# u read to all partitions by one DMA and kept as bf16, in a linear-attention and long-convolution kernel with a new instruction order

## The chip, the cores and the metric

The kernel runs on one core of a Trainium2 chip. The metric is the device time of one launch in microseconds, as the median over several runs. A core has five engines that work at the same time, each through its own list of instructions in order: PE (TensorE, matmuls), DVE (VectorE), ACT (ScalarE), POOL (GpSimd) and SP (SyncE, which here issues every DMA). Matmul results land in PSUM, which POOL can't read; all else lies in SBUF.

## What is computed

The inputs r, k, v and w have the shape 4 x 8 x 768 x 48 (batch, heads, steps, width of a head), and u is 8 x 48. For each batch and head a 48 x 48 state runs through the steps, and its output goes through a projection, a circular convolution over the 768 steps with a gate on each side, and an output projection:

```
cur   = outer(u * k[t], v[t])
y[t]  = r[t] @ (state + cur)
state = w[t][:, None] * state + outer(k[t], v[t])
...
x1, x2, x3 = split(x @ w_proj)          # x is y with the heads side by side, 768 x 384 per batch
out = (x1 * irfft(rfft(x2) * rfft(filter)) * x3) @ w_out
```

The term with u, called the bonus here, is v[t] times one number per step and head: the sum over the head's width of r[t] * k[t] * u.

## The kernel before

The 768 steps of a batch are cut into six chunks of 128 steps, so there are 24 chunks, numbered 0 to 23 through the four batches. A chunk's r, k, v and w come by one DMA each (ldr, ldk, ldv, ldw), 128 partitions (the steps) by 384 values, of which each run of 48 lies apart in memory. Six buffers of each are used in turn.

Work on a chunk c, by the names of the functions (op_ left out): lw takes the logarithm of w on ACT. cs and ce add it up over the steps by matmuls with a triangular mask (inclusive and exclusive). en and eq, or enp and eqp, which write back into PSUM, take exponentials on ACT. kh or khp makes k times the one and q or qp makes r times the other, on DVE or POOL; those with a p read PSUM and are DVE's. tqk transposes both on PE, tT copies the result, sc multiplies them into scores, and mt masks these on DVE (or ma copies them on ACT and mm masks them on POOL). kv and S carry the state. rk is r * k in bf16, rku is rk * u, cc sums rku over each head on DVE, and vc is v * cc on POOL: the bonus. y multiplies the scores with v and adds the state's share; yb also adds vc by an identity matmul, and its result is copied out by xc, where after a plain y the addition is done by xn on DVE. yt transposes, and xT copies the transposed chunk.

Work on a batch b: sa and sb add and subtract the two halves of the sequence, x2 projects them, ab copies. f does a discrete Fourier transform by matmuls with a table F, in six slots f.b.0 to f.b.5. da and db (or X, ua and ub) multiply the slots with the filter's transform T, pp adds, i1 and i2 transform back, ec, s and d put the halves together. p1 and p3 are the other two projections, taken up by x1 and g (or gc and gm). yy multiplies, po (in the last batch poa and pob) projects the output, o copies it, and st stores it.

Set-up: iota, ang and sin make F. Of these, ang writes into o0 but reads a ramp that lies in the tile `filt`, so the filter's own load (ldfilt) waits until ang and angn are done. fs and fd add and subtract the halves of the filter, hf transforms them (slots 0 and 1 need fs alone, 2 and 3 both, 4 and 5 fd), and ht, hr, he and hb make T from that with small rotations (rot, which rsc scales). mtr, mc and ms make the tables for the way back. ldp loads a third of the projection weights (ldp1 for x2, ldp0 for p1, ldp2 for p3) or the output weights (ldp3), and wc converts them to bf16. z and zs are matmuls on a zero tile whose results aren't used.

u is loaded by ldu (L371) as one row on one partition. us (L324) spreads it to 128 partitions by a matmul with a row of ones, and uc (L328) copies this from PSUM into u_bc, which is FP32 (L193); rku (L552) reads u_bc. um (L331), uv (L339) and hm (L315) make a second form of u that only the functions rt, rT, cu and cv (L559 to L576) read, the bonus by PE. None of these four stands in the order.

The order of everything is the string ORDER (L37 to L129). Each word names an engine, a function and its numbers, and for PE a PSUM bank: `V:rku0`, `A:lw1`, `P:ce1@2`. emit (L855) walks through it, and each engine does its words in this order, waiting only where data or a buffer demands it. One further wait is written in: a POOL word with a `!` waits for the last DVE word ahead of it that is in the set `shut` (L851), which holds operations on SBUF alone. The document calls this wait a turn. Loads and stores are words of SP, so they too go in this order.

Of the kernel before, what the change touches and what calls it, by code (L numbers as in the profile page):

```python
# [42 lines left out]
V:hr0.0 A:ht0.1 A:enp2 G:q1! V:hr0.1 V:tT0 V:rku1 P:zs8@2 P:hf3@0 A:ht1.0 A:he G:v0! P:z2@2 P:mtr0@2
G:rk2! A:ht1.1 A:mc0 P:tqk1@3 P:hf4@1 P:sc0@8 V:hr1.0 V:hr1.1 G:vc0! V:cc1 V:khp2 S:ldr3 S:ldv1
P:kv0@5 A:tT1 A:lw3 V:rku2 G:v1! P:z3@0 P:cs3@4 V:S0 S:ldk3 P:mtr1@0 V:q2 P:ce3@3 A:ht2.1 A:ms0
A:en3 G:kh3! A:eq3 S:ldw4 P:tqk2@2 G:rk3! V:hb0 P:kv1@3 P:hf5@4 V:cc2 A:mc1 A:lw4 A:ht2.0 A:tT2
V:mt0 G:vc1! S:ldw5 S:ldv2 S:ldr4 V:hr2.1 A:lw5 P:sc1@8 S:ldk5 P:zs2@1 P:ce4@5 S:ldk4 P:z3@1 V:S1
A:hb1 V:mt1 G:rku3! P:cs4@3 G:q3! A:eqp4 V:hr2.0 P:zs2@2 P:sc2@8 A:v2 V:mt2 P:cs5@2 S:ldv3 V:qp4
P:yb0@1 A:en5 G:vc2! V:cc3 P:kv2@4 A:en4 A:xc0 P:tqk3@2 A:ph4 G:rk4! P:yt0@1 P:mtr2@3 P:yb1@5 A:tT3
P:sc3@8 P:zs2@2 P:yb2@2 V:kh4 V:S2 V:ms2 P:tqk4@4 G:rku4! S:ldv5 S:ldw6 G:kh5! A:v3 A:mc2 A:xc1  # L50
P:ce5@5 A:xT0 A:hb2 A:eqp5 V:mt3 V:cc4 V:tT4 S:ldv4 P:zs1@1 A:lw6 P:yt1@3 P:kv3@1 A:ms1 G:v5! G:v4!
P:sc4@8 P:ce6@0 S:ldr5 G:rk5! S:ldw8 S:ldr6 V:S3 A:xc2 A:xT1 V:qp5 P:tqk5@2 P:yt2@5 P:kv4@3 A:lw8
A:eq6 S:ldk6 G:vc4! P:ce8@1 P:cs6@4 G:rku5! V:mt4 P:yb4@0 A:tT5 V:S4 S:ldw7 P:sc5@8 A:enp6 A:xc4
G:q6! A:lw7 P:zs1@2 P:cs8@3 V:cc5 A:eq8 A:en8 P:y3@2 V:khp6 G:vc5! S:ldp1 V:xT2 G:vc3! V:mt5 P:yt4@0
# [6 lines left out]
A:tT7 V:S6 P:y6@3 A:v7 V:da0.2 P:cs9@0 G:rk8! A:en9 A:x10.1.0 P:f0.5@2 A:wc2 P:p10.1.1@1 G:vc7!
V:da0.1 V:xn6 V:db0.2 S:ldk9 V:rku8 P:yt6@3 P:p10.0.0@0 P:ce9@5 P:kv7@2 P:sc7@8 A:xT6 V:ub0.1
P:p10.2.0@4 V:pp0.2 V:pp0.1 V:rk9 V:pp0.0 A:eq9 A:x10.0.0 A:x10.2.0 P:p30.1.1@3 A:x10.1.1 P:tqk8@5
A:ma7 V:rku9 G:q9! G:mm7! S:ldk10 V:g0.1.1 P:p30.1.0@0 V:g0.1.0 S:ldv8 V:cc8 P:p30.0.0@4 S:ldw10
V:cc9 V:g0.0.0 A:tT8 A:v8 V:S7 P:i20.2@1 S:ldw11 P:i10.2@3 S:ldr10 P:p10.0.1@0 P:p30.2.0@5 P:sc8@8
P:yb7@4 S:ldr11 A:lw10 A:ec0.2 V:g0.2.0 P:cs10@2 S:ldw12 S:ldv9 G:kh9! S:ldv10 S:ldk11 A:x10.0.1
S:ldw14 G:vc8! S:ldv11 A:lw11 P:kv8@0 P:ce10@5 S:ldk12 S:ldv12 P:i20.1@1 V:d0.2 V:mt8 A:en10 A:xc7
P:ce11@2 P:tqk9@4 A:eq10 S:ldr12 A:ec0.1 A:eqp11 V:s0.2 V:S8 G:rk10! P:y8@5 P:i20.0@1 G:q10! P:yt7@3
S:ldw13 V:xn8 G:kh10! P:i10.1@0 V:qp11 A:tT9 S:ldp3 A:ec0.0 P:sc9@8 A:xT7 V:s0.1 G:rku10! S:ldk13
A:v9 S:ldk14 S:ldv13 S:ldr13 G:vc9! S:ldr14 A:lw12 S:ldw15 P:yt8@2 S:ldw16 S:ldv14 V:d0.1 S:ldk15  # L70
S:ldw17 S:ldr15 P:tqk10@1 A:tT10 P:cs11@3 A:enp11 P:i10.0@4 V:mt9 P:kv9@0 V:xT8 S:ldr16 V:S9
P:p30.0.1@5 P:yb9@1 G:rk11! V:cc10 A:v10 A:xc9 G:yy0.1! P:ce12@2 P:p11.1.0@0 A:eq12 V:khp11
P:p30.2.1@1 P:tqk11@2 P:cs12@3 V:g0.0.1 V:d0.0 P:sc10@8 P:yt9@5 A:x11.1.0 A:lw14 A:v11 A:en12 A:tT11
V:g0.2.1 V:s0.0 P:p11.0.0@0 P:ce14@3 V:sb9 A:eq14 A:v12 P:kv10@4 P:p11.2.0@1 G:vc10! G:rku11!
P:p31.2.0@2 G:kh12! A:x11.2.0 V:mt10 S:ldk16 V:sa9 V:xT9 V:cc11 V:S10 P:yb10@3 G:yy0.2! A:lw13
A:gc1.2.0 A:xc10 V:rk12 S:ldv15 S:ldr17 S:ldk17 S:ldw18 P:x21.1.0@5 A:x11.0.0 V:q12 V:rku12 P:cs14@1
P:ce13@2 S:ldw19 P:yt10@3 P:sc11@8 P:p31.0.0@0 P:cs13@4 A:ab1.1.0 A:eq13 G:vc11! P:x21.0.0@2 V:sb10
G:yy0.0! P:p31.1.0@5 V:mt11 V:sa10 A:xT10 V:g1.1.0 A:en13 A:ab1.0.0 P:tqk12@4 P:y11@2 A:wc3 V:g1.0.0
A:enp14 P:x21.1.1@3 S:ldw20 V:xn11 V:khp14 V:cc12 P:po0.4@5 P:po0.1@0 A:tT12 G:kh13! P:kv12@2
G:rk13! P:po0.5@1 V:S12 V:q14 A:ab1.1.1 A:o0.1 P:yt11@4 A:xT11 V:rku13 V:q13 A:o0.5 A:lw15 P:po0.0@3  # L80
V:sb11 V:sa11 P:tqk14@0 P:p11.0.1@2 P:tqk13@1 S:ldv16 P:sc12@8 G:vc12! P:x21.0.1@4 G:rk14! G:v14!
A:v13 V:tT14 S:ldk18 P:kv13@0 A:o0.4 A:x11.0.1 G:rku14! V:mt12 P:cs15@2 P:x21.0.2@5 V:cc13 A:tT13
A:o0.0 S:ldr18 G:vc13! V:S13 P:ce15@1 A:lw16 A:en15 P:sc13@8 P:po0.3@3 A:eq15 P:kv14@2 P:ce16@0
P:x21.1.2@1 S:ldv17 V:mt13 A:ab1.0.1 P:sc14@8 G:kh15! P:yb13@4 A:lw17 A:o0.3 G:q15! S:ldk20 V:S14
S:ldv18 A:ab1.1.2 P:ce17@1 P:y12@3 A:eq16 P:f1.5@0 G:rk15! V:cc14 S:ldk19 S:ldr20 G:vc14! V:mt14
P:tqk15@2 A:xc13 A:eq17 S:ldr19 V:xn12 A:ab1.0.2 G:rk16! G:q16! S:ldw21 P:cs17@1 P:f1.1@4 P:cs16@3
P:f1.2@5 V:db1.2 S:ldv19 A:tT15 V:db1.0 P:yb14@2 V:da1.1 A:enp16 A:en17 A:xc14 P:p31.2.1@0 P:sc15@8
V:khp16 V:rku15 V:rku16 P:yt14@2 P:yt13@5 P:yt12@1 P:f1.4@4 A:xT14 S:ldk21 A:xT12 A:xT13 P:f1.0@2
A:v15 P:p31.0.1@1 A:gc1.2.1 S:ldr21 P:p32.1.0@5 P:p11.1.1@0 P:p12.2.0@3 V:gm1.2.0 V:da1.2 V:cc15
A:lw19 V:g1.0.1 P:cs19@1 P:f1.3@4 A:lw18 A:gc2.1.0 A:x11.1.1 A:en19 A:x12.2.0 A:lw20 V:da1.0 G:rk17!  # L90
V:mt15 P:p32.0.0@2 G:pp1.2! P:tqk16@0 A:tT16 G:kh17! G:q17! A:v16 P:kv15@1 P:p12.0.0@3 P:p11.2.1@5
A:x12.0.0 V:db1.1 P:tqk17@4 V:rku17 A:tT17 V:pp1.0 V:pp1.1 P:sc16@8 P:po0.2@0 V:S15 P:cs18@3 A:en18
G:vc15! V:g2.0.0 V:cc16 P:ce18@1 P:i21.2@4 P:cs20@3 P:kv16@2 V:mt16 A:eq18 A:ec1.2 V:cc17 G:rk18!
A:en20 S:ldw23 S:ldk22 P:y15@1 G:q18! P:i21.1@4 S:st0.3 S:ldv20 A:x11.2.1 P:sc17@8 P:i21.0@5 G:vc16!
P:ce20@3 V:xn15 V:S16 A:v17 A:ec1.1 V:mt17 P:y16@4 P:yt15@2 A:o0.2 A:ec1.0 V:sa15 G:kh18! V:xT15
V:xn16 A:eq20 P:ce19@0 S:ldw22 P:p32.2.0@5 P:p31.1.1@3 P:y17@1 A:eq19 A:v18 V:g2.2.0 P:tqk18@0
A:tT18 G:kh20! P:yt16@4 V:sb15 G:q20! S:st0.0 S:ldr22 P:i11.1@5 P:x22.0.0@2 V:rku18 G:vc17! A:xT16
S:ldr23 S:ldv22 S:st0.1 S:ldv21 A:ab2.0.0 A:lw21 V:g1.1.1 S:ldv23 S:ldk23 G:rk19! S:st0.4 G:kh19!
V:sb16 P:tqk20@3 P:kv18@0 V:d1.1 P:sc18@8 P:x22.1.1@2 V:sa16 V:s1.1 V:xn17 G:rku19! A:tT20 P:i11.2@4
P:x22.0.1@5 P:yt17@3 V:S18 V:cc18 A:ab2.1.1 V:s1.2 A:v19 A:xT17 P:x22.1.0@0 G:q19! P:i11.0@2  # L100
A:ab2.1.0 A:ab2.0.1 V:sb17 V:d1.2 P:p32.1.1@1 P:ce21@0 P:p12.1.1@5 A:x12.1.1 V:sa17 P:x22.0.2@3
P:cs21@4 A:gc2.1.1 V:mt18 G:rk21! G:rk20! G:vc18! V:d1.0 V:s1.0 A:eq21 V:cc19 P:sc20@8 A:en21 A:lw23
V:yy1.1 V:gm1.2.1 P:x22.1.2@5 P:kv19@1 A:ab2.0.2 V:S19 P:p32.2.1@2 A:gc2.2.1 G:kh21! G:rku20!
P:p32.0.1@4 P:y18@3 A:ab2.1.2 P:tqk19@0 A:v20 V:mt20 A:tT19 A:lw22 P:p12.1.0@5 A:gc2.0.1 P:f2.3@1
P:p12.0.1@2 V:xn18 P:yt18@3 P:sc19@8 A:x12.0.1 A:xT18 A:x12.1.0 P:kv20@0 V:yy1.0 V:yy1.2 P:f2.1@4
P:ce22@2 A:eq22 V:db2.1 V:S20 V:cc20 P:po1.5@3 P:cs23@1 A:en23 V:db2.0 G:q21! P:po1.0@0 P:cs22@2
A:enp22 A:o1.5 P:po1.3@5 V:mt19 P:y20@1 G:rku21! G:vc20! P:tqk21@4 P:f2.4@3 A:o1.0 P:po1.1@0 V:xn20
# [804 lines left out]
```

## Time and profile before

| | |
|---|---|
| median of 3 runs | 158.15 us (158.08 to 158.39) |
| the profiled execution | 159.17 us |
| its span, from the first to the last instruction | 157.5 us |
| mean granted clock of PE | 0.98 of full speed |
| ACT busy | 128.0 us |
| read from memory | 22.41 MB |
| written to memory | 4.72 MB |

How to read the lines of the profile in what follows. In a table of groups each row is a line of the kernel, an engine, an operation and its tiles (output <- inputs, with buffer numbers left out) and the count, then the busy time in us and the mean of one in ns, then the idle time of the engine just before them with what ended most of it. The types in a row are those of the output and of one input only. In a list in order of time a row begins with the start and the duration in us. In the chain of waits (the chain of work that ended last, followed back from the end) a row is a start, a duration and what was done. In a list of waits a row gives who waited for whom, the sum in us, how many times, and the longest. PE's ends are modelled, since matmuls overlap; the chain's durations don't overlap.

### The profile page before, as it was taken

What the parts mean: (1) busy time and instruction counts of PE and PEld (TensorE: products, weight loads), DVE (VectorE), ACT (ScalarE), POOL (GpSimd) and SP (SyncE); (2) the same over time, 40 slices, a digit from 0 to 9 for tenths busy, and PEclk for the clock granted to TensorE, in tenths of its full rate; (3) what the DMA queues carried; (4) which work ended last, traced back from release to release, by engine and by line L of the source; (5) the groups of instructions that cost most, each with busy time, mean ns of one, the idle gap of its engine ahead of it and who ended that gap; (6) DMA issues with size and microseconds to landing.
All of it is one profiled execution on the core that took longest, in us unless ns stands there. A gap on an engine that the chain in (4) does not pass through costs nothing.

```text
span 157.5 us, 4173 instructions
## 1 busy us (share of the span) xinstructions
PE 143.3 (91%) x1553; PEld 92.6 (59%) x1553; DVE 139.1 (88%) x254; ACT 128.0 (81%) x264; POOL 108.7 (69%) x147
## 2 busy tenths in 40 slices
...
GB/s 100 187 320 209 151 201 208 216 172 249 232 176 266 163 211 219 142 251 183 204 229 190 174 205 184 205 242 195 251 14 152 0 102 2 0 0 91 234 241 190
...
## 3 DMA queue, kind: packets, MB, share of 16 engines
...
q8 instruction: 12, 0.20, 0.5%
q14 instruction: 8, 0.07, 0.1%
HBM read 22.41 MB, written 4.72 MB: 172 GB/s over the span
## 4 chain that ended last, share of the span: by engine, by line
PE 46%; DVE 4%; ACT 2%; issue 1%; ACTq 0%
PE p L699 10%; PE po L812 8%; PE i L770 5%; PE f L431 4%; PE x L730 3%; PE tqk L588 3%; PE sc L601 2%; PE f L424 2%; PE y L654 2%; PE yt L677 1%; PE y L649 1%; PE ce L495 1%; PE kv L629 1%; PE cs L489 1%; ACT xT L235 1%; PE kv L627 1%
## 5 line engine op out<-in xcount | busy, mean ns | idle before, releaser
L699 PE MATMUL p<-xT,wproj 128*128 128x384 bf16 x144 | 28.9, 326 | 0.0
L608 DVE TENSOR_TENSOR mt<-sc,mask_excl 128x1024 bf16<-128x1024 f32 x21 | 25.5, 1213 | 0.0
L582 POOL TENSOR_TENSOR vc<-v,cc 128x384 bf16<-128x384 bf16 x24 | 19.9, 831 | 7.3 <-DVE P L764 3.0
L547 POOL TENSOR_TENSOR qk<-ldr,eq 128x384 bf16<-128x384 f32 x16 | 16.1, 1003 | 11.2 <-ACT eq L514 5.5
L550 POOL TENSOR_TENSOR rk<-ldr,ldk 128x384 bf16<-128x384 f32 x21 | 20.9, 1001 | 3.9 <-DMA ldr<-in_r_dram 2.1
L235 ACT ACTIVATE qkT<-tqk 128x1024 bf16<-128x1024 bf16 x21 | 21.7, 1034 | 1.3 <-PE tqk L588 1.2
L699 PEld LDWEIGHTS <-wproj 128*128 128x128 bf16 x144 | 12.7, 97 | 8.2 <-issue 0.8
L588 PE MATMUL tqk<-ident,qk 128*128 128x128 bf16 x192 | 14.8, 219 | 2.6 <-DVE qk L547 1.8
L543 POOL TENSOR_TENSOR qk<-ldk,en 128x384 bf16<-128x384 f32 x14 | 14.0, 1005 | 3.0 <-DVE g L725 1.5
L485 ACT ACTIVATE lg<-ldw 128x384 bf16<-128x384 f32 x24 | 12.8, 539 | 3.9 <-DMA ldw<-in_w_dram 3.7
L730 PE MATMUL x<-wproj,sd 128*128 128x384 bf16 x72 | 14.5, 326 | 1.1 <-POOL wproj L236 0.6
L588 PEld LDWEIGHTS <-qk 128*128 128x128 bf16 x192 | 12.0, 97 | 4.7 <-DVE qk L547 2.0
L770 PE MATMUL i<-m_b,P 128*128 128x384 bf16 x72 | 14.6, 326 | 0.0
L812 PE MATMUL po<-wout,y 128*128 128x384 bf16 x72 | 14.3, 326 | 0.0
L235 ACT ACTIVATE x<-p 128x384 bf16<-128x384 f32 x24 | 11.8, 505 | 2.8 <-PE p L699 2.7
L556 DVE TENSOR_REDUCE cc<-rku 128x8 f32<-128x384 bf16 x24 | 12.8, 540 | 0.1
L235 ACT ACTIVATE xT<-yt 128x384 bf16<-128x384 bf16 x19 | 9.1, 496 | 4.3 <-DVE sd L686 2.8
L514 ACT ACTIVATE eq<-ce 128x392 f32<-128x392 f32 (+1 forms) x20 | 10.0, 504 | 2.2 <-POOL v L236 1.5
L235 ACT ACTIVATE ab<-x 128x384 bf16<-128x384 f32 x23 | 11.1, 496 | 0.8 <-PE x L730 0.6
L758 DVE TENSOR_TENSOR UA<-f,T 128x768 bf16<-128x768 f32 x12 | 11.2, 947 | 0.1
L637 DVE TENSOR_TENSOR S<-kv,eq 128x384 bf16<-128x384 f32 x20 | 10.9, 546 | 0.3 <-PE kv L629 0.3
L601 PE MATMUL sc<-qkT 48*128 48x128 bf16 x192 | 9.5, 218 | 1.2 <-DVE mt L608 0.8
...
## 6 DMA issues: line engine op xcount, KB each, us to landing
ldw<-in_w_dram SPq DMA_DIRECT2D x24, 192.0 KB, 3.8
ldr<-in_r_dram SPq DMA_DIRECT2D x24, 192.0 KB, 3.9
ldk<-in_k_dram SPq DMA_DIRECT2D x24, 192.0 KB, 4.1
ldv<-in_v_dram SPq DMA_DIRECT2D x24, 192.0 KB, 3.8
out_dram<-o SPq DMA_DIRECT2D x12, 192.0 KB, 2.7
out_dram<-filt SPq DMA_DIRECT2D x12, 192.0 KB, 2.6
...
```

Of the source, the lines that this page charges most:

```text
L235: return nc.scalar.activation(out=o, in_=i, func=AF.Copy)
L485: nc.scalar.activation(out=lg_b[c % 3][:, :, 0:D], in_=ld["w"][c % LD], func=AF.Ln)
L543: return two(e).tensor_mul(qk_b[c % 3][:, 1, :, 0:D], ld["k"][c % LD], en_b[c % 3])
L547: return two(e).tensor_mul(qk_b[c % 3][:, 0, :, 0:D], ld["r"][c % LD], eq)
L550: return two(e).tensor_mul(rk_b[c % 2], ld["r"][c % LD], ld["k"][c % LD])
L582: return two(e).tensor_mul(vc_b[c % 3], v_b[c % 4], cc_b[c % 3].to_broadcast([L, H, D]))
L588: nc.tensor.transpose(p[:, x, j, :], qk_b[c % 3][:, x, 2 * j:2 * j + 2, :], ident)
L608: nc.vector.tensor_mul(mt_b[c % 3], bank_of[f"sc{c}"].rearrange("p q j t -> p (q j) t"), dataclasses.replace(m[:, :], ap=[m[:, :].ap[0], [ ...
L699: nc.tensor.matmul(p, wproj[:, n, cb, fb * L:(fb + 1) * L], xT_b[b % 2][:, cb, sl], start=(cb == 0), stop=(cb == CB - 1),)
L730: nc.tensor.matmul(p, sd_b[q][:, cb, ti * L:(ti + 1) * L], wproj[:, 1, cb, :], start=(cb == 0), stop=(cb == CB - 1),)
L770: nc.tensor.matmul(p, P_b[b % 2][:, s // 2, s % 2, cb * L:(cb + 1) * L], m_b[:, s].rearrange("p a t -> p (a t)"), start=(i == 0), stop=(i ...
L812: nc.tensor.matmul(p, y_b[0][:, cb, ti * L:(ti + 1) * L], wout[:, cb, :], start=(cb == FIRST[0]), stop=(cb == FIRST[-1]),)
```

## The change

u is now read by one DMA whose source has a step of 0 over 128 partitions, so that each partition gets all 384 values. uc converts this tile to bf16, on POOL, and u_bc is bf16. us, um, uv and hm are gone, with the row of ones, the tiles of the bonus by PE and its four functions. uc joins the set of operations that take turns.

```
-    u_row = consts.tile([1, C], FP32)
-    one_row = consts.tile([1, L], FP32)
-    hm = consts.tile([L, CB, H], BF16)
-    uh = consts.tile([L, CB, H], BF16)
-
-    u_bc = consts.tile([L, H, D], FP32)
+    u_all = consts.tile([L, C], FP32)
+
+    u_bc = consts.tile([L, H, D], BF16)
...
     def op_uc(e, k_):
-        copy(e, u_bc.rearrange("p h d -> p (h d)"), bank_of["us"])
...
+        return copy(e, u_bc.rearrange("p h d -> p (h d)"), u_all)
...
     def op_ldu(e, k_):
-        nc.sync.dma_start(out=u_row, in_=dataclasses.replace(u, ap=[[C, 1], [1, C]]))
+        nc.sync.dma_start(out=u_all, in_=dataclasses.replace(u, ap=[[0, L], [1, C]]))
...
     shut = {"kh", "q", "rk", "rku", "vc", "v", "ua", "ub", "pp", "yy", "gm", "wc",
-            "fs", "fd", "hb", "ang", "angn", "he"}
+            "fs", "fd", "hb", "ang", "angn", "he", "uc"}
```

The whole of ORDER is new: 1,093 words became 1,088. It has the same work on the chunks and batches, but many words have another place, and some another engine or form. rku stands 9 times on DVE (14 before) and 15 times on POOL (10). On DVE there are also fewer fd (it is POOL's now), rk, q, xT, gm, kh, ab, ub and pp, and more mc, ms, khp, yy, db, mt, xn and copies; all small memsets are DVE's. The z and zs have the same number of matmuls in all. The set-up begins:

```
-V:mem0 G:iota! P:zs29@0 V:ang2 S:ldw1 V:ang0 V:ang1 A:tLn G:iorot! A:lw1 S:ldw0 V:mem3 S:ldu S:ldr0
-S:ldk0 S:ldfilt G:mem6! G:mke! G:mem2! G:mem4! V:angn G:mkd! G:mem1! S:ldw2 G:mki! S:ldk1 A:lw0
-G:mem5! S:ldw3 P:us@0 S:ldr1 P:um@1 P:z1@2 P:ce1@2 V:uc V:rk0 P:cs1@0 G:hm! S:ldv0 V:rku0 P:z5@3
-A:sin S:ldk2 P:ce0@4 A:eq0 A:eq1 A:lw2 V:uv V:fs S:ldr2 P:cs0@3 P:z7@5 A:enp0 A:enp1 V:fd V:rsc
...
+S:ldw0 V:mem0 G:iorot! G:mke! G:iota! P:zs29@0 A:tLn S:ldw2 A:lw0 S:ldw1 S:ldr0 G:mki! S:ldk0 A:lw2
+S:ldu V:mem2 V:mem4 V:mem3 V:ang1 V:mem1 V:ang2 V:ang0 A:lw1 V:angn P:cs0@0 P:ce0@1 P:z3@2 P:z7@3
+A:enp0 P:ce1@2 S:ldfilt A:eq0 P:zs1@3 G:mkd! G:rk0! G:uc! S:ldk2 P:zs8@1 V:mem5 V:rku0 V:khp0 P:z2@3
+P:cs1@1 A:sin P:cs2@4 P:z1@3 V:q0 S:ldk1 P:zs1@5 V:fs S:ldv0 A:enp2 A:ph1 A:enp1 P:zs2@3 P:zs2@5
+P:tqk0@5 V:mem6 G:fd! P:hf0@3 V:rsc V:cc0 V:khp2 P:mtr0@0 P:hf1@4 A:tT0 A:ht0.0 P:ce2@5 P:sc0@8
+A:ms0 V:khp1 V:mc0 A:eqp1 V:hr0.0 S:ldr1 S:ldw3 G:rk1! S:ldr2 A:ht0.1 A:v0 P:mtr2@0 S:ldk3 V:qp1
+S:ldr3 P:hf2@1 G:vc0! V:mc2 A:ht1.0 A:eq2 P:tqk1@2 P:kv0@3 G:q2! G:rk2! V:ms2 V:hr0.1 S:ldv1 A:lw3
```

and where the first p1 stands (p10.2.1 before, p10.1.0 after):

```
-P:x20.1.2@1 A:ab0.1.2 A:wc0 P:f0.0@3 P:f0.1@4 P:tqk7@1 P:f0.4@0 A:ma6 V:cc7 G:mm6! S:ldp2 G:q8!
-A:lw9 P:kv6@2 P:p10.2.1@5 V:da0.0 S:ldr9 A:x10.2.1 V:db0.0 P:f0.3@3 P:f0.2@4 P:p10.1.0@5 A:X0.3
...
+P:x20.1.2@0 G:rk7! V:mt6 S:ldk8 G:kh7! P:f0.0@5 A:ab0.1.2 V:cc6 V:db0.0 S:ldv7 A:eq8 V:rku7 P:kv6@4
+P:f0.4@3 V:S6 P:f0.5@0 A:wc0 P:f0.2@1 G:vc6! G:kh8! V:da0.2 P:tqk7@4 V:db0.2 V:cc7 V:da0.0 G:v7!
+S:ldr8 P:p10.1.0@3 G:rk8! P:p10.2.0@2 P:kv7@0 A:tT7 S:ldw10 A:x10.2.0 V:S7 P:p10.1.1@4
```

205 lines of the change are left out of this document (83 added, 122 removed).

## Prediction, written before the result

> **What bounds the kernel now.** I read the page's busy times first, then the stretches of ten microseconds, then the chain of waits, and last what DVE waited for.
>
> ```profile
> PE 143.3 (91%) x1553; PEld 92.6 (59%) x1553; DVE 139.1 (88%) x254; ACT 128.0 (81%) x264; POOL 108.7 (69%) x147
> ```
>
> The span is 157.5 us. PE and DVE are both near full on average, which says little. The stretches say which is full where (PE, PEld, DVE, ACT, POOL busy, then clock, DMA share, GB/s):
>
> ```profile
> 20.00:30.00 10.00, 7.02 (x107) 4.92 (x103) 9.71 (x16) 7.60 (x17) 8.30 (x11) 1.00 1.04 206
> 30.00:40.00 10.00, 8.95 (x155) 6.83 (x152) 9.25 (x18) 9.60 (x22) 8.58 (x11) 1.00 0.96 205
> 40.00:50.00 10.00, 9.65 (x79) 5.82 (x79) 9.81 (x17) 8.73 (x17) 8.27 (x10) 1.00 0.97 232
> 60.00:70.00 10.00, 9.00 (x114) 6.16 (x114) 10.00 (x21) 8.87 (x20) 8.89 (x9) 1.00 0.89 196
> 70.00:80.00 10.00, 9.12 (x104) 6.22 (x104) 8.17 (x17) 8.80 (x20) 5.95 (x6) 1.00 1.02 206
> 80.00:90.00 10.00, 10.00 (x133) 6.51 (x130) 10.00 (x16) 9.02 (x21) 8.26 (x11) 1.00 1.00 193
> ```
>
> From 20 to 70 us DVE has almost nothing idle while PE loses 2.98, 1.05, 0.35 and 1.00 us in the stretches shown, and the DMA engines are full as well (share 0.96 to 1.04 up to 50). From 80 us PE is full. The chain agrees:
>
> ```profile
> PE 46%; DVE 4%; ACT 2%; issue 1%; ACTq 0%
> ...
> 84.47 0.49 PE f L431 x3
> ```
>
> Its last half is PE work end to end, one forward group costing 0.49 us. So the end moves only if PE gets through its list sooner, and it can do that only before about 80 us, in places where it waits for DVE or for the loads. Before 20 us DVE mostly waits for the set-up:
>
> ```profile
> 10.99 1.36 DVE L414 TENSOR_TENSOR UA<-filt 128x1152 bf16<-128x1152 f32 x1 [2.50 <-DMA filt<-in_moe_filter_fft_dram]
> ...
> DVE u_bc L236 <- PE us L326: 0.9, 1, 0.9
> DVE uh L340 <- POOL hm L318: 0.5, 1, 0.5
> ```
>
> **The change: u.** The two matmul steps, the copy from PSUM, hm and uv go. All that sat ahead of the filter's landing at 10.99, and DVE waited 2.50 us there all the same. So I cost their going at nothing: the filter's load covers it, and were that cover gone it would be worth 1.4 us (the 0.9 and 0.5 above). What counts is bf16:
>
> ```profile
> L553 DVE TENSOR_TENSOR rku<-rk,u_bc 128x384 bf16<-128x384 bf16 x14 | 9.4, 682 | 1.3 <-POOL rk L550 1.2
> L553 POOL TENSOR_TENSOR rku<-rk,u_bc 128x384 bf16<-128x384 bf16 x10 | 9.2, 922 | 0.7 <-PE y L654 0.7
> L725 DVE TENSOR_TENSOR g<-g,x 128x384 bf16<-128x384 bf16 x6 | 2.0, 352 | 0.4 <-ACT x L235 0.4
> ...
> L553 DVE TENSOR_TENSOR rku<-rk,u_bc x14: 543/550/1337, 7.3 to 126.6; 128x384 bf16<-128x384 bf16 x14
> ```
>
> The rku row's input type is rk's; u_bc was FP32. The same shape with all of it bf16 (L725) takes 352 ns against a median of 550. The mean, 682, is 132 above the median: some wait inside the instruction. The new list has 9 rku on DVE, not 14 (15 on POOL). With the 132 kept: 14 x 0.682 = 9.55 us becomes 9 x 0.484 = 4.36, that is -5.2 us on DVE. If bf16 bought nothing it would be 9 x 0.2 = 1.8 us less of a gain. The Trainium skill (VectorE: DVE Perf Modes, section The TRN2 errata) would have 58 cycles and half an element's cycle each, an estimate of (58 + 192) / 0.96 = 260 ns and so another 0.8 us of gain; the 352 ns row speaks against it.
>
> **The change: the order on DVE.** I counted the words of both lists by engine and priced them by these rows:
>
> ```profile
> L417 DVE TENSOR_TENSOR UA<-filt 128x1152 bf16<-128x1152 f32 x1 | 1.4, 1352 | 0.0
> L761 DVE TENSOR_TENSOR UB<-f,T 128x768 bf16<-128x768 f32 x9 | 8.5, 949 | 0.3 <-PE f L431 0.2
> L531 DVE TENSOR_TENSOR qk<-cs,ldk 128x384 bf16<-128x384 f32 x9 | 4.9, 549 | 0.3 <-ACT cs L521 0.2
> L804 DVE TENSOR_TENSOR y<-SD,g 128x768 bf16<-128x768 bf16 x8 | 4.6, 610 | 0.1
> L608 DVE TENSOR_TENSOR mt<-sc,mask_excl 128x1024 bf16<-128x1024 f32 x21 | 25.5, 1213 | 0.0
> L236 DVE COPY xT<-yt 128x384 bf16<-128x384 bf16 x5 | 1.7, 346 | 0.0
> L550 DVE TENSOR_TENSOR rk<-ldr,ldk 128x384 bf16<-128x384 f32 x3 | 1.7, 579 | 0.0
> L764 DVE TENSOR_TENSOR P<-UA,UB 128x768 bf16<-128x768 bf16 x10 | 5.2, 549 | 0.0
> ```
>
> rku -5.2; fd to POOL -1.35; da and db together one more, +0.95; khp three more, +1.65; yy three more, +1.83; mt one more, +1.21; mc and ms four more at xT's price, +1.38; xT four fewer, -1.38; rk two fewer, -1.16; q two fewer at khp's price, -1.10; pp, ua and ub together two fewer, -1.10; gm two fewer, -0.70. The rest are single moves: eight PSUM or float operations at 0.55 (xc, xn, ec, o, qp in; g, kh, ab out) and sa for v, together +1.1. Sum -3.9 us. The memsets that come to DVE lie ahead of the filter, in idle time. There also lies khp0 and q0 now (0.55 each) where rk0 and a dearer rku0 lay: another -0.3. So behind the filter's landing DVE has 4.2 us less to do.
>
> **The start and the loads.**
>
> ```profile
> 5.13 0.37 SPq L375 DMA_DIRECT2D filt<-in_moe_filter_fft_dram  x1
> ...
> 39.03 1.14 POOL L236 CAST wproj<-o 128x1152 bf16<-128x1152 f32 x1 [1.17 <-DMA o<-in_moe_w_proj_dram]
> ...
> 44.44 1.16 ACT L235 ACTIVATE wproj<-o 128x1152 bf16<-128x1152 f32 x1 [0.60 <-DMA o<-in_moe_w_proj_dram]
> ...
> ldw<-in_w_dram SPq DMA_DIRECT2D x24, 192.0 KB, 3.8
> ```
>
> Adding up the loads in the list's order, the filter ended at 1,922 KB and came at 10.99; the first projection block ended at 7,298 KB and came at 39.03: 192 KB per us, or 1.0 us per load of 192 KB. In the new list one more such load and u, now 196 KB, go ahead of the filter. u comes in 128 rows of 1,536 B, and no row shows such a load; it costs between nothing and 1.0 us, and I take 0.3, near the low end, as its pieces are eight times a load's 192 B. The filter is also issued behind the angles on DVE, which get later, as POOL makes iota third instead of first; that is hidden as long as the queue is still draining. Filter: +1.3, between +1.0 and +2.0. Behind it in SP's queue stand ldk2, ldk1 and ldv0, with all later loads.
>
> On DVE that leaves -4.2 + 1.3 = -2.9 us. But PE has a gate of its own. The second block, wproj0, which every p1 needs, stands at 8,450 KB before and 8,525 KB after, so with DMA full it comes 0.4 us later, not sooner. By the lists and the chain's prices the PE work behind the first p1 is 1.0 us shorter in the new order: two more forward groups, f0.5 and f0.2, stand ahead of it (2 x 0.49; f0.0, f0.1 and f0.4 stood there already), and little else changes but one bonus matmul fewer. v5 now ends at 6,989 KB, by the pace at 37.4, early enough for these groups. So at the first p1: -1.0 + 0.4 = -0.6. From there PE can still win what it loses until 80 us, and the chain shows how it loses it:
>
> ```profile
> 71.19 1.21 DVE mt L608
> 72.39 0.27 DVE sd L686
> ...
> 73.14 0.49 ACT en L507
> 73.67 0.61 PE tqk L588 x8
> ```
>
> ACT is late for PE there because DVE is late for ACT. Of the 1.00 and 0.88 us lost between 60 and 80, I take half as won by a DVE whose list behind the first p1 has got some 5 us shorter: -1.0, between nothing and -2.0. Sum: -0.6 - 1.0 = **-1.6 us**, inside the 2.9 that DVE allows.
>
> On POOL the set-up evens out (fd in, the memsets and hm out); the rest of the list is about 3 us longer: five rku, two rk, three gm and one pp in, three yy and two kh out. The turns by which POOL waits for DVE are fewer: 22 DVE operations that some POOL step waits for become 16. POOL isn't full, so I cost both at nothing; the cover is its idle time of 1.11, 4.05 and 1.74 us in the three stretches from 60.
>
> The profiled run took 159.17 us, 1.7 more than its span, and the median of the runs is 158.15; I take 1.6 off both: 157.6 and 156.55, rounded to 156.5.
>
> **Rivals.** *The port's wait takes the place of the filter's (158.2).* DVE's two-input operations stretch where POOL works:
>
> ```profile
> 20.29 1.17 DVE L553 TENSOR_TENSOR rku<-rk,u_bc 128x384 bf16<-128x384 bf16 x1 [1.04 <-POOL rk L550]
> ...
> 20.22 0.83 POOL L582 TENSOR_TENSOR vc<-v,cc 128x384 bf16<-128x384 bf16 x1
> ```
>
> The new list puts fd on POOL right behind fs on DVE, and rsc, a small product of two SBUF tiles, behind fs and two memsets on DVE, with no turn between rsc and fd. fd would take some 3 us:
>
> ```profile
> L550 POOL TENSOR_TENSOR rk<-ldr,ldk 128x384 bf16<-128x384 f32 x21 | 20.9, 1001 | 3.9 <-DMA ldr<-in_r_dram 2.1 <-DVE g L725 1.7
> L804 POOL TENSOR_TENSOR y<-SD,g 128x768 bf16<-128x768 bf16 x4 | 6.6, 1647 | 1.1 <-DVE y L804 1.1
> ...
> 53.07 0.54 DVE L553 TENSOR_TENSOR rku<-rk,u_bc 128x384 bf16<-128x384 bf16 x1
> ...
> 53.75 1.00 POOL L547 TENSOR_TENSOR qk<-ldr,eq 128x384 bf16<-128x384 f32 x1 [3.36 <-DVE rku L553]
> ```
>
> Three times rk gives 3.0, one and a half times yy 2.5. POOL starts 0.14 us after the DVE operation it waited for (53.61 to 53.75); DVE needs about as long for two memsets, so who is first is open. If it is fd, rsc ends 3 us late, and behind it all that needs rot (ht on ACT, hr) and cc0, khp2, khp1 on DVE: -2.9 + 3.0 = +0.1. The Trainium skill (SBUF — State Buffer, section SBUF: two separate sides) says it outright: the pair of ports shared by VectorE and GpSimd is held for a whole instruction, and the loser blocks. By that rule the stretch above is no accident; 1.17 us beside an 0.83 us vc agrees with it.
>
> *POOL becomes the bound between 50 and 95 us (159.5).* If its turns don't let it use its idle time, the 3 us more come through, net -1.6 + 3.0 = +1.4. It decides once POOL's busy time in the stretches from 60 to 90 comes near 10, where it is 8.89, 5.95 and 8.26 now. Against it: fewer turns.
>
> *All of DVE's saving comes through (155.2).* The gate at wproj0 eases because SP issues sooner when buffers come free sooner: -2.9. The 2.98 and 1.05 us that PE loses from 20 to 40 have room for it.
>
> *bf16 doesn't shorten rku, or its wait sets its end (158.2).* 1.8 us come back. L725 speaks against it.
>
> **The numbers.** Forecast 0.42; all of DVE's saving 0.15; the port 0.20; POOL 0.15; bf16 0.08. What this kernel's measurement can tell from no change is 0.2%, 0.3 us. The port and bf16 cases lie around no change by a us or so, since the forecast's own unknowns (u 0 to 1.0, filter +1.0 to +2.0) hold there too; I split their 0.28 into 0.07 faster, 0.10 same and 0.11 slower. Faster 0.42 + 0.15 + 0.07 = 0.64, same 0.10, slower 0.15 + 0.11 = 0.26. The range goes from 154.6, beyond the full DVE saving by half of u's and the filter's spread, to 159.5, the POOL case, and leaves out about 2 in 10; the forecast's own is 155.4 (half of u's spread below -2.6) to 157.8 (-0.6, and the rest of the filter's).
>
> **What would show it.** Right: rku on DVE near 0.35 to 0.5 us; the filter about 1.3 later; wproj0's conversion still near 44 to 45 with f0.5 and f0.2 ahead of the first p1; PE idle of about 1 us between 60 and 80, and PE full from there. Wrong: rsc lasting 2.5 to 3 us beside fd; POOL near 10 from 60 to 90; or a PE wait behind hf2, which needs fd and now stands in front of tqk1 and kv0.

## The result and the profile after

The changed kernel took 159.11 us as the median of 4 runs (159.05 to 159.36), the kernel before 158.12 (157.93 to 158.39) on the same chip. The ratio is 1.0064, with an interval of 1.0046 to 1.0083: slower by 0.64%, some 1.0 us, where I had forecast 1.6 us faster. One caution on the traces: the execution of before that the prediction quotes took 159.17 us, about 1 us above the median of its timed runs, while the one of after (159.13 us, span 157.4) is an ordinary one. The spans of these two are alike (157.5 and 157.4 us) and show nothing of the difference, so I compare after with the experiments below as well.

The busy times of after, from its page:

```profile
PE 142.6 (91%) x1541; PEld 92.8 (59%) x1544; DVE 136.6 (87%) x264; ACT 126.0 (80%) x261; POOL 111.0 (71%) x134
```

DVE was busy for 2.5 us less and POOL for 2.3 us more. Yet the end is later. What happened in the start stands in the list in order of time of DVE, with POOL's and SP's rows of the same stretch (start, duration, what it was, then the idle time before it and what ended it):

```profile
10.83 0.36 DVE L524 TENSOR_TENSOR rku<-rk,u_bc 128x384 bf16<-128x384 bf16 x1 [5.19 <-POOL u_bc L232]
...
13.87 1.36 DVE L385 TENSOR_TENSOR UA<-filt 128x1152 bf16<-128x1152 f32 x1 [1.74 <-DMA filt<-in_moe_filter_fft_dram]
...
15.38 2.56 DVE L340 TENSOR_TENSOR rot<-rot,rsc 128x12 f32<-128x12 f32 x1
```

```profile
10.30 0.50 POOL L232 CAST u_bc<-u_all 128x384 bf16<-128x384 f32 x1 [1.79 <-DMA u_all<-in_u_dram]
...
15.31 2.61 POOL L388 TENSOR_TENSOR UA<-filt 128x1152 bf16<-128x1152 f32 x1 [4.51 <-DVE UA L385]
```

```profile
4.62 0.70 SPq L343 DMA_DIRECT2D u_all<-in_u_dram  x1
5.44 0.37 SPq L346 DMA_DIRECT2D filt<-in_moe_filter_fft_dram  x1
5.85 1.63 SPq L450 DMA_DIRECT2D ldk<-in_k_dram  x2
7.53 6.16 SPq L450 DMA_DIRECT2D ldv<-in_v_dram  x1
13.73 0.63 SPq L450 DMA_DIRECT2D ldr<-in_r_dram  x1
```

Two things are to be seen. The filter came in at 13.87 us where it came in at 10.99 before, 2.88 us later and not 1.3. And rsc, a product of 12 numbers per partition, took 2.56 us beside POOL's fd: the port's wait that I had only as a rival. In SP's rows the chunk loads stand still behind ldv0, whose issue lasts 6.16 us: the next load, ldr1, goes out at 13.73.

The page's issue rows say what one load of u costs (KB, then us from issue to landing):

```profile
filt<-in_moe_filter_fft_dram SPq DMA_DIRECT2D x1, 1152.0 KB, 8.4
o<-in_moe_w_out_dram SPq DMA_DIRECT2D x1, 576.0 KB, 5.8
u_all<-in_u_dram SPq DMA_DIRECT2D x1, 192.0 KB, 5.6
```

A third of the bytes took nearly as long as the 576 KB of the output weights. The stretches of after (columns as before) show the place and what PE made of it:

```profile
7.00:9.00 2.00, 2.00 (x21) 1.23 (x20) 0.00 (x0) 1.99 (x3) 1.00 (x1) 1.00 0.80 140
9.00:11.00 2.00, 1.60 (x14) 0.87 (x12) 0.17 (x1) 1.98 (x5) 0.50 (x1) 1.00 0.99 323
```

```profile
10.00:15.00 5.00, 1.45 (x14) 0.81 (x13) 2.43 (x4) 3.79 (x7) 0.50 (x1) 0.87 0.89 242
15.00:20.00 5.00, 2.62 (x11) 1.42 (x11) 4.50 (x8) 1.96 (x5) 3.56 (x2) 0.50 1.11 217
```

From 7 to 9 us the DMA engines are busy for 0.80 of the time and move 140 GB/s; two microseconds later, at 0.99, 323. PE then has little to do until the filter is there and taken up; its granted clock is 0.87 from 10 to 15 us and 0.50 from 15 to 20.

Behind the filter the two kernels also wait for different things. In the list of waits from 20 to 62 us (who waited for whom, the sum in us, how many times, the longest) before has these waits for loads:

```profile
POOL rk L550 <- DMA ldr<-in_r_dram: 1.5, 1, 1.5
POOL wproj L236 <- DMA o<-in_moe_w_proj_dram: 1.2, 1, 1.2
ACT wproj L235 <- DMA o<-in_moe_w_proj_dram: 0.9, 2, 0.6
POOL v L236 <- DMA ldv<-in_v_dram: 0.2, 1, 0.2
```

The same list of after, which goes down to 0.2 us, has no wait for a load at all. What keeps the pace there is the engines' own lists, POOL's among them: from 30 to 40 us it is busy for the whole 10.00 us (8.58 before), and the chain of waits runs through it until it converts the first projection block.

```profile
30.00:40.00 10.00, 9.36 (x145) 6.91 (x146) 9.87 (x18) 9.72 (x21) 10.00 (x12) 1.00 1.00 219
```

```profile
38.34 0.91 POOL rku L524
39.25 1.10 POOL wproj L232
40.39 0.65 PE x L682 x3
```

### The profile page after: what moved, and what is told of

Read it like the earlier page. It is cut to its first block, busy times and chain, and to the rows that moved or that the text cites. A ratio compares the mean times of both kernels' runs of the same rounds, so it can differ in the third digit from the quotient of the medians.

```text
span 157.4 us, 4146 instructions
## 1 busy us (share of the span) xinstructions
PE 142.6 (91%) x1541; PEld 92.8 (59%) x1544; DVE 136.6 (87%) x264; ACT 126.0 (80%) x261; POOL 111.0 (71%) x134
## 4 chain that ended last, share of the span: by engine, by line
PE 58%; ACT 10%; DVE 8%; DMA 8%; POOL 5%; issue 5%; SPq 3%; ACTq 0%; DVEq 0%; POOLq 0%
PE p L651 13%; PE x L682 6%; PE po L764 6%; DMA ldk<-in_k_dram 5%; PE f L402 5%; PE tqk L540 4%; PE i L722 4%; PE sc L553 3%; PE f L395 3%; SPq L450 2%; DMA ldw<-in_w_dram 2%; PE y L606 2%; PE ce L466 2%; DVE rot L340 2%; ACT xT L231 2%
## 5 line engine op out<-in xcount | busy, mean ns | idle before, releaser
L521 POOL TENSOR_TENSOR rk<-ldr,ldk 128x384 bf16<-128x384 f32 x23 | 23.0, 1002 | 7.4 <-DMA ldk<-in_k_dram 3.1
L560 DVE TENSOR_TENSOR mt<-sc,mask_excl 128x1024 bf16<-128x1024 f32 x22 | 26.7, 1216 | 0.5 <-PE sc L553 0.4
L518 POOL TENSOR_TENSOR qk<-ldr,eq 128x384 bf16<-128x384 f32 x17 | 17.0, 1001 | 3.0 <-ACT eq L485 3.0
L540 PE MATMUL tqk<-ident,qk 128*128 128x128 bf16 x192 | 15.4, 223 | 1.1 <-DVE qk L502 1.1
L682 PE MATMUL x<-wproj,sd 128*128 128x384 bf16 x72 | 15.0, 326 | 1.0 <-ACT ab L231 0.6
L524 POOL TENSOR_TENSOR rku<-rk,u_bc 128x384 bf16<-128x384 bf16 x15 | 13.7, 915 | 2.7 <-DVE y L756 1.5
L514 POOL TENSOR_TENSOR qk<-ldk,en 128x384 bf16<-128x384 f32 x12 | 12.0, 1002 | 2.4 <-ACT x L231 2.0
L231 ACT ACTIVATE xT<-yt 128x384 bf16<-128x384 bf16 x23 | 11.0, 494 | 1.0 <-DVE sd L638 0.8
L710 DVE TENSOR_TENSOR UA<-f,T 128x768 bf16<-128x768 f32 x11 | 10.4, 949 | 0.3 <-PE f L395 0.3
L677 POOL TENSOR_TENSOR g<-g,x 128x384 bf16<-128x384 bf16 x8 | 7.2, 913 | 4.7 <-DVE g L677 2.6
```

What stands on the lines that cost most here:

```text
L231: return nc.scalar.activation(out=o, in_=i, func=AF.Copy)
L518: return two(e).tensor_mul(qk_b[c % 3][:, 0, :, 0:D], ld["r"][c % LD], eq)
L521: return two(e).tensor_mul(rk_b[c % 2], ld["r"][c % LD], ld["k"][c % LD])
L524: return two(e).tensor_mul(rku_b[c % 2], rk_b[c % 2], u_bc)
L540: nc.tensor.transpose(p[:, x, j, :], qk_b[c % 3][:, x, 2 * j:2 * j + 2, :], ident)
L560: nc.vector.tensor_mul(mt_b[c % 3], bank_of[f"sc{c}"].rearrange("p q j t -> p (q j) t"), dataclasses.replace(m[:, :], ap=[m[:, :].ap[0], [ ...
```

## The experiments

Three theories are named in the expectations. START: what is lost in the set-up (rsc's wait, u's load) goes to the end. LIST: the new list is worse further on. STREAM, formed after the first four runs: up to about 60 us the loads, in SP's order, set the pace. All ratios are to the kernel before on the same chip; e1 to e4 ran on one chip, e5, e6, e7 and e9 on another, e8 and e10 to e15 on a third, e16 and e17 on a fourth. Each interval reaches about 0.0035 to both sides (0.006 in e8, with 6 runs), so two kernels whose ratios differ by less than about 0.005 (0.8 us) are not told apart.

| run | median us | ratio | interval |
|---|---|---|---|
| e1 before's order, u by one DMA, bf16 | 159.51 | 1.0096 | 1.0056 to 1.0136 |
| e2 before, u_bc in bf16 | 158.05 | 1.0005 | 0.9970 to 1.0041 |
| e3 after, rsc ahead of fs | 159.03 | 1.0043 | 1.0006 to 1.0080 |
| e4 after, u as a row and a matmul | 156.93 | 0.9954 | 0.9917 to 0.9992 |
| e5 e4, rsc ahead of fs | 156.79 | 0.9910 | 0.9876 to 0.9944 |
| e6 e4, u's load to 128 partitions, unused | 159.14 | 1.0093 | 1.0062 to 1.0124 |
| e7 e6 from 128 different rows | 157.38 | 0.9978 | 0.9940 to 1.0016 |
| e8 e5 with fillers | 156.50 | 0.9847 | 0.9789 to 0.9905 |
| e9 e4, half of the filter | 155.03 | 0.9836 | 0.9792 to 0.9880 |
| e10 after, u's load by ACT | 158.85 | 1.0016 | 0.9981 to 1.0051 |
| e11 e4, u_bc in FP32 | 157.72 | 0.9953 | 0.9918 to 0.9988 |
| e12 e6 to 32 partitions | 157.58 | 0.9941 | 0.9907 to 0.9974 |
| e13 after with fillers | 159.43 | 1.0056 | 1.0020 to 1.0092 |
| e14 e4 with fillers | 156.77 | 0.9909 | 0.9875 to 0.9944 |
| e15 e6 to 64 partitions | 157.45 | 0.9965 | 0.9935 to 0.9996 |
| e16 e6, the unused load behind the filter's | 157.65 | 0.9981 | 0.9950 to 1.0012 |
| e17 e4, 576 KB more behind the filter's | 158.45 | 1.0013 | 0.9976 to 1.0050 |

**The change in parts: e1 to e4.** e1 keeps before's order without the words us, um, uv and hm, and takes the new load and the bf16 tile; e2 only sets the type of u_bc; e3 moves one word of after; e4 takes u back to a row and a matmul.

```
 e2
-    u_bc = consts.tile([L, H, D], FP32)
+    u_bc = consts.tile([L, H, D], BF16)
 e3
-P:cs1@1 A:sin P:cs2@4 P:z1@3 V:q0 S:ldk1 P:zs1@5 V:fs S:ldv0 A:enp2 A:ph1 A:enp1 P:zs2@3 P:zs2@5
-P:tqk0@5 V:mem6 G:fd! P:hf0@3 V:rsc V:cc0 V:khp2 P:mtr0@0 P:hf1@4 A:tT0 A:ht0.0 P:ce2@5 P:sc0@8
+P:cs1@1 A:sin P:cs2@4 P:z1@3 V:q0 S:ldk1 P:zs1@5 V:rsc V:fs S:ldv0 A:enp2 A:ph1 A:enp1 P:zs2@3 P:zs2@5
+P:tqk0@5 V:mem6 G:fd! P:hf0@3 V:cc0 V:khp2 P:mtr0@0 P:hf1@4 A:tT0 A:ht0.0 P:ce2@5 P:sc0@8
 e4
-A:enp0 P:ce1@2 S:ldfilt A:eq0 P:zs1@3 G:mkd! G:rk0! G:uc! S:ldk2 P:zs8@1 V:mem5 V:rku0 V:khp0 P:z2@3
+A:enp0 P:ce1@2 P:us@4 S:ldfilt A:eq0 P:zs1@3 G:mkd! G:rk0! S:ldk2 P:zs8@1 V:mem5 V:uc V:rku0 V:khp0 P:z2@3
...
-        nc.sync.dma_start(out=u_all, in_=dataclasses.replace(u, ap=[[0, L], [1, C]]))
+        nc.sync.dma_start(out=u_row, in_=dataclasses.replace(u, ap=[[C, 1], [1, C]]))
```

> The order of before with only the four words of the old spreading taken out; u comes by the one DMA to 128 partitions and u_bc is bf16. Theory START (the loss is made in the set-up of the changed kernel, by rsc's wait of 2.4 us beside fd and by u's load, which puts the filter off by some 1.9 us): here no rsc wait, but u's load delays the filter from 11.0 to 12.5-13 us, and 14 cheaper rku give it back: 157.3 to 158.5 us. Theory LIST (the new list is worse later on, the start doesn't matter): 156.3 to 157.2 us, the pure gain of bf16.

> The kernel before with u_bc in bf16 and nothing else. 14 rku on DVE at 0.35 instead of 0.55 us are 2.8 us less on DVE. Both theories: 156.3 to 157.3 us if DVE bounds up to 80 us, as the prediction had it; 158.0 to 158.3 us if a wait sets the end of rku or if PE and the loads hold the time anyway.

> The changed kernel with the one word rsc put ahead of fs on DVE, where POOL has nothing to do. START: rsc takes 0.16 us instead of 2.56, the mask of chunk 3 comes about 2.4 us sooner, and the time falls by 1 to 2.4 us, to 156.7 to 158.1. LIST: chunk 3 comes sooner but the time stays at 158.8 to 159.3.

> The changed kernel with u again read as one row and spread by one matmul, copied from PSUM to bf16 by DVE. START: the filter lands at about 12 us instead of 13.9, rku0 no longer waits until 10.8, and the time falls by 0.8 to 1.9 us, to 157.2 to 158.3. LIST: 158.8 to 159.3.

e2 does what I priced: rku's row on DVE becomes

```profile
L553 DVE TENSOR_TENSOR rku<-rk,u_bc 128x384 bf16<-128x384 bf16 x14 | 4.9, 356 | 1.9 <-POOL rk L550 1.9
```

that is 356 ns where it had 682, 4.5 us less on DVE. The time doesn't move (1.0005). e1 differs from e2 mostly by u's load, and is 1.0096 - 1.0005 = 0.9%, 1.4 us, slower (0.6 to 2.3 by the intervals). So the load, and not the new order, is what costs. In this order, where it is the third load to be issued, it puts the filter off by less: the filter comes at 12.00 us in e1, at 11.38 in e2 and at 10.99 in before. How 0.6 to 1.0 us there become 1.4 at the end was not followed up. e4 shows the load's price from the other side: without it the new order is at 0.9954, and 1.0064 / 0.9954 says that the load costs it 1.7 us (1.0 to 2.4). The rows of e4 against those of after:

```profile
11.70 1.36 DVE L391 TENSOR_TENSOR UA<-filt 128x1152 bf16<-128x1152 f32 x1 [1.39 <-DMA filt<-in_moe_filter_fft_dram]
...
13.21 2.56 DVE L346 TENSOR_TENSOR rot<-rot,rsc 128x12 f32<-128x12 f32 x1
```

```profile
46.86 1.14 PE L657 MATMUL p<-xT,wproj 128*128 128x384 bf16 x6
...
145.55 1.14 PE L728 MATMUL i<-m_b,P 128*128 128x384 bf16 x6
```

In after the same two groups on PE stand at

```profile
49.03 1.14 PE L651 MATMUL p<-xT,wproj 128*128 128x384 bf16 x6
...
147.72 1.14 PE L722 MATMUL i<-m_b,P 128*128 128x384 bf16 x6
```

The filter is 13.87 - 11.70 = 2.17 us later in after, the first p1 is 2.17 later, and a group near the end is 2.17 later. Nothing in between takes any of it back. LIST is out. (e4's list of waits from 20 to 62 us has no wait for a load either.) rsc took 2.56 us in e4 as well, so its wait isn't the cause either; e3, where rsc comes first and takes 0.16 us,

```profile
12.37 0.16 DVE L340 TENSOR_TENSOR rot<-rot,rsc 128x12 f32<-128x12 f32 x1
```

gains 0.2%, which isn't told from nothing. In its trace the mask of chunk 3 starts 2.37 us sooner than in after (20.29 for 22.66), but the first p1 only 0.87 sooner (48.16 for 49.03). What e3 wins on DVE it gives back waiting for loads; from its chain of waits:

```profile
33.08 2.98 SPq L450
36.11 5.45 DMA ldw<-in_w_dram
41.58 0.52 ACT lg L456
```

The issue of a chunk load on SP lasts 2.98 us, ldw goes out behind it, and the logarithm waits for ldw.

**DVE or the loads: e5, e9, e11.** e5 is e4 with e3's move; e11 is e4 with u_bc in FP32; e9 leaves out half of the filter:

```
-            out=filt, in_=moe_filter_fft.rearrange("(n p) c -> p n c", p=L)
+            out=filt[:, 0:NT, :], in_=moe_filter_fft[0:NT * L, :].rearrange("(n p) c -> p n c", p=L)
...
-filt[:, 0:NT, :], filt[:, NT:, :]
+filt[:, 0:NT, :], filt[:, 0:NT, :]
```

> The kernel of e4 (new order, u as one row and a matmul) with the word rsc moved ahead of fs. STREAM (up to about 60 us the loads in SP's order set the pace, so time gained on DVE in the set-up is given back while waiting for loads; u's load of 192 KB delays all behind it): the mask of chunk 3 comes about 2.5 us earlier than in e4, and the end within 0.5 us of e4, 156.5 to 157.3 us. START (the end follows what DVE loses in the set-up): 2.4 us off, 154.5 us.

> The kernel of e4 with only the first half of the filter loaded (576 of 1,152 KB), and that half used in place of the second too, which leaves half of the filter out. STREAM: the load ahead of everything is 576 KB lighter, 2.3 us at 250 KB a us, so the end is 1.8 to 2.6 us ahead of e4, 154.3 to 155.1 us. If the loads do not set the pace: within 0.5 us of e4.

> The kernel of e4 with u_bc in FP32 instead of bf16, so that DVE's nine rku take about 0.68 instead of 0.35 us, 3.0 us more on DVE, and POOL's fifteen whatever they do. STREAM: within 0.4 us of e4, 156.6 to 157.3 us. My ledger of DVE (DVE's time goes to the end from 20 to 70 us): five of the nine lie there, 1.6 us later, 158.3 us or more.

e9 comes at 0.9836, 1.2% or 1.9 us ahead of e4, as STREAM said: half the bytes ahead of everything, and the gain is there at the end. It doesn't single out STREAM, though, since the filter too is there sooner (DVE takes it up at 10.64 us). e5's 0.4% isn't told from e4. In e11 DVE's rku take 5.5 us instead of 3.9,

```profile
L530 DVE TENSOR_TENSOR rku<-rk,u_bc 128x384 bf16<-128x384 bf16 x9 | 5.5, 621 | 0.1
```

and the ratio is e4's, 0.9953. So bf16, which the prediction called what counts, is worth nothing that can be told in the new order either.

**What is dear in u's load: e6, e7, e12, e15, e10.** e6, e7, e12 and e15 add to e4 a load whose result nobody reads, right behind u's:

```
 e6
+    def op_ldx(e, k_):
+        nc.sync.dma_start(out=u_all, in_=dataclasses.replace(u, ap=[[0, L], [1, C]]))
...
-S:ldu
+S:ldu S:ldx
 e7
+        nc.sync.dma_start(out=u_all, in_=moe_w_out[0:L, :])
 e12
+        nc.sync.dma_start(out=u_all[0:32, :], in_=dataclasses.replace(u, ap=[[0, 32], [1, C]]))
```

e15 has 64 for the 32. e10 is after with the load issued by ACT, as its first word.

> The kernel of e4 (u as one row, spread by a matmul) with one more load right behind u's, whose result nobody reads: u's row read to all 128 partitions, the change's own load. STREAM: the filter lands 2.0 to 2.3 us later than in e4 and the end is later by the same, 158.9 to 159.3 us, as in after. START or the order alone (the load costs only through those who wait for u): within 0.5 us of e4, 156.5 to 157.4 us.

> As e6, with the same bytes in packets of the same size (128 of 1,536 B), but from 128 different rows of the output weights instead of 128 times u's row. If it is the bytes that delay the stream, at about 250 KB a us: 0.8 us later than e4, 157.7 us, and if every extra load costs the same whatever it reads, as e6. If reading one row 128 times is what is slow: well below e6, and its packets take 65 ns or so where u's took 107 to 182 ns.

> The kernel of e6 (a dead load of u's one row beside the row and the matmul) with 32 partitions instead of 128, 48 KB in 32 packets. If each repeated reading of the row has its price: a quarter of e6's 2.2 us over e4, 0.5 us, 157.3 us. If the load has a price of its own, whatever its size: near e6, 158.5 us or more.

> The kernel of e6 (a dead load of u's one row beside the row and the matmul) with 64 partitions instead of 128. If the price grows in proportion: 1.1 us over e4, 158.0 us. If the first readings are covered by the slow start that the filter's own first packets show, and the rest is paid in full: 0.3 to 0.8 us over e4, 157.2 to 157.7 us.

> The kernel of after with u's load issued first of all by ACT instead of by SP between ldk0 and ldfilt: another queue, and its time falls on w's, r's and k's first loads. If the reading of one row holds only its own queue: the filter lands near 12 us as in e4 and the end is 156.9 to 157.5 us. If it slows all that the core loads meanwhile, whatever the queue: the first chunk's loads come later instead, the filter lands at 13 to 14 us, and the end stays at 158.7 to 159.3 us.

e6 is 1.4%, 2.2 us, slower than e4, though nothing waits for its load. The same bytes in the same pieces from 128 different rows (e7) cost 0.2%, not told from nothing, and by the intervals at most 0.8%, 1.2 us. e6 and e7 ran on the same chip, and between them lie 1.15%, 1.8 us (1.0 to 2.6). The issue rows of u_all in e6, e7, e12 and e15:

```profile
u_all<-in_u_dram SPq DMA_DIRECT2D x1, 192.0 KB, 5.2
```

```profile
u_all<-in_moe_w_out_dram SPq DMA_DIRECT2D x1, 192.0 KB, 2.7
```

```profile
u_all<-in_u_dram SPq DMA_DIRECT2D x1, 48.0 KB, 2.5
```

```profile
u_all<-in_u_dram SPq DMA_DIRECT2D x1, 96.0 KB, 3.1
```

128 different rows land in 2.7 us, one row 128 times in 5.2. From 7 to 9 us e6, then e7, then e4 move (the last two numbers are the DMA share and GB/s)

```profile
7.00:9.00 2.00, 2.00 (x21) 1.19 (x19) 0.42 (x1) 1.99 (x2) 0.99 (x1) 1.00 0.63 128
```

```profile
7.00:9.00 2.00, 2.00 (x20) 1.18 (x18) 0.56 (x1) 1.97 (x3) 0.99 (x1) 1.00 0.91 248
```

```profile
7.00:9.00 2.00, 2.00 (x19) 1.21 (x19) 0.56 (x1) 1.99 (x3) 0.99 (x1) 1.00 0.86 270
```

128 GB/s against 248 and 270. So most of the price is neither the bytes nor the size of the pieces but the reading of one row of 1,536 B over and over, and it holds up what comes behind it. The bytes may have a share: in e7's traced execution, at 158.56 us 1.2 above its median, the filter comes at 13.25 us, between e4's 11.70 and e6's 14.31. 32 and 64 readings cost -0.1% and +0.1%, by the intervals at most 0.6 and 1.0 us. The 0.5 us that I had expected for 32 isn't ruled out by that; the 1.1 us that a proportion would give for 64 is. In e10 the load went out at 0.80 us on ACT's queue; the filter still landed at 13.67 and the end is 0.5% ahead of after, about the least that can be told, where e4 is 1.1% ahead. By these ratios another queue takes less than half of the price away; the intervals allow anything from 0.1 to 1.4 us of it. The Trainium skill (DMA: Bandwidth & Descriptors, section Issuing engines are not separate DMA queues) says that loads started by different engines end up on the same 16 DMA engines and interleave; e10's filter agrees.

**The clock: e8, e13, e14.** Twelve filler matmuls on PE while it waits for the filter, in e5, after and e4:

```
-P:hf0@3
+P:z12@3 P:hf0@3
```

> The kernel of e5 with twelve filler matmuls of 512 columns on PE ahead of hf0, where PE idles for the filter and the granted clock falls to 0.50 in 15 to 20 us. If the lost clock costs time up to the end: the clock stays above 0.8 in 15 to 20 us and the end is 0.5 to 1.5 us ahead of e5, 155.3 to 156.3 us. STREAM (PE waits for the loads there anyway): within 0.3 us of e5, whatever the clock.

> The kernel of after with twelve filler matmuls of 512 columns ahead of hf0, so that PE does not idle while the filter comes. If the lost clock (0.50 in 15 to 20 us) carries part of what after loses: the clock stays near 1.00 there and the end comes 0.7 us or more ahead of after, 158.4 us or less. STREAM alone: within 0.4 us of after, 158.7 to 159.5 us.

> The kernel of e4 with the same twelve fillers ahead of hf0. If the clock has a price of its own: 0.7 us or more ahead of e4, 156.2 us or less. STREAM alone: within 0.4 us of e4, 156.5 to 157.3 us.

In e13 the clock from 15 to 20 us is

```profile
15.00:20.00 5.00, 3.55 (x24) 1.84 (x22) 4.90 (x9) 1.71 (x4) 3.57 (x2) 0.98 0.98 193
```

0.98 instead of 0.50, and the time is after's (1.0056 against 1.0064). The lost clock isn't what after lost. In e13's trace the first p1 does come sooner behind the filter, 33.76 us (47.87 - 14.11) for after's 35.16, but from there to the end of the span it takes 109.9 us for 108.4; and from 20 to 62 us its list of waits has loads again, 4.3 us in all. e14 against e4 isn't told apart. Only e8, with rsc first and the clock held, lies wholly below e4 by its interval: that speaks for the two together being worth something once u's load is gone, but it rests on 6 runs, isn't told from e5 or e14, and by the medians (156.50 against 158.25 on that chip, 0.989) would be too little to tell. At either figure e8 beats both kernels.

**The filter or the loads behind it: e16, e17.** In all runs so far both move together. e16 puts e6's unused load behind ldfilt; e17 puts there an unused load of half of the filter's rows, 576 KB:

```
-S:ldfilt
+S:ldfilt S:ldx
```

> The kernel of e6 with the dead load of u's row to 128 partitions right behind the filter's in SP's list instead of ahead of it. The filter lands as in e4, near 11.7 us; the loads from ldk2 on come 1 to 2.2 us later than in e4. STREAM (chunk loads set the pace): the end is later by about as much as ldr1 is issued later, 158 to 159.2 us. If it is the filter's landing that the end follows: within 0.4 us of e4, 156.5 to 157.3 us.

> The kernel of e4 with one more dead load right behind the filter's: half of the filter's 1,152 KB a second time, in packets of 1,536 B, 576 KB in all. The filter lands near 11.7 us; the loads behind come about 2.5 us later than in e4, at 230 KB a us. STREAM: 1.9 to 2.6 us later than e4, 158.8 to 159.5 us, the mirror of e9. If the end follows the filter's landing: within 0.4 us of e4.

SP's rows give the time at which ldr1 goes out: 11.43 in e4, 12.53 in e16 and 13.49 in e17:

```profile
13.49 0.68 SPq L460 DMA_DIRECT2D ldr<-in_r_dram  x1
```

In e17 the filter lands at 12.04, 0.34 later than in e4, the loads behind it go out 2.06 later, and the end is 0.6% later, 0.9 us (0.1 to 1.8 by the intervals): less than the 1.9 to 2.6 us expected. e16: 1.10 later, and 0.3%, not told from nothing. So STREAM as I had put it, that the loads alone set the pace, falls too.

The traces say where each limit holds. From the filter to the first p1 it takes 35.16 us in after and in e4, 35.21 in e6, 35.17 in e10, and also 34.99 and 35.17 in e16 and e17 with their late loads (35.54 in e7, and 35.77 in e11, whose rku take longer). The first p1 of e17:

```profile
47.21 1.14 PE L661 MATMUL p<-xT,wproj 128*128 128x384 bf16 x6
```

Up to there the engines' lists behind the filter set the pace in these kernels, and the filter's delay is handed on whole. In e17 the rest is lost behind the first p1 (109.7 us to the end of the span for e4's 108.0). Its list of waits from 46 to 72 us names loads, where those of after, e4 and e6 name none:

```profile
POOL qk L528 <- DMA ldr<-in_r_dram: 1.0, 1, 1.0
ACT lg L466 <- DMA ldw<-in_w_dram: 0.9, 2, 0.7
```

In e3 and e13, where the lists get on faster, waits for loads come up too, 3.9 and 4.3 us from 20 to 62. That fits two limits close to each other, the engines' lists behind the filter and the loads, of which the later one counts; in after it is the lists. The filter late and the loads on time was not run.

## Right or wrong, point by point

*The sum.* It had three terms: 0.4 us lost at the first p1 by the loads, 1.0 us less work for PE behind it, and 1.0 won between 60 and 80 us. The two behind the first p1 came. PE's idle time from 60 to 80 us fell from 1.88 us (1.13 in e2's trace) to 0.64, by 0.5 to 1.2. From the first p1 to the end of the span it takes 108.4 us in after, for 111.8 in before's trace and 110.6 in e2's, 2.3 to 3.5 less, where 2.0 was forecast. What failed is the first term. The first p1 of before stands at

```profile
45.66 0.66 PE L699 MATMUL p<-xT,wproj 128*128 128x384 bf16 x3
```

and after's at 49.03, 3.37 later and not 0.4.

*u's matmuls, copy, hm and uv at nothing.* Right: they lay in the wait for the filter, and so does the new wait of 5.19 us for u.

*bf16.* The size was right and a little small: 408 ns for the 484 that I took, 356 in e2. Its worth was overrated: DVE's saving by itself moved nothing that can be told (e2, e11). In e2 some 5 us of waits for loads stand between 20 and 62 us.

*u's load.* The step that failed: "it costs between nothing and 1.0 us, and I take 0.3, near the low end, as its pieces are eight times a load's 192 B." By the words of the new list the second projection block stands at 8,640 KB with u's 192 KB and at 8,448 without, for 8,450 before. The prediction's 8,525 thus gives u's load 77 KB, and all of the 0.4 us at the first p1 is u's load. What the runs showed in its place: the filter and the first p1 are both 2.17 us later in after than in e4. At the end the load costs 1.4 us in the old order, 1.7 in the new, and 2.2 as an unused load. I priced bytes and pieces, and e7 shows that these are the smaller part. I had no row of a row read many times, and closed the range at the price of an ordinary load, where nothing bounded it above. The other 1.2 us by which the first p1 is late (46.86 in e4 for 45.66) are not u's load; where they come from stays open.

*The filter's landing.* 1.3 us later was forecast, 1.0 of it for one more chunk load and 0.3 for u; 2.88 came. Of it 0.71 is left in e4 (11.70), and the 2.17 are u's load. I let this delay act on DVE's saving alone; the first p1 hung on it as well.

*The gate and the order.* wproj0's conversion, forecast near 44 to 45 us, stands in after and in e4 at

```profile
47.26 1.21 ACT L231 ACTIVATE wproj<-o 128x1152 bf16<-128x1152 f32 x1
```

```profile
45.09 1.21 ACT L232 ACTIVATE wproj<-o 128x1152 bf16<-128x1152 f32 x1
```

Neither row names a wait, where before's names 0.60 us for the load. So in the new order this block is no gate by its load: ACT comes to it in its own list, 2.17 us later with u's load than without. That e4's 45.09 lies near the forecast is luck. Without u's load the new order with bf16 gives 0.7 us by the ratio of e4, whose interval reaches from 0.1 to 1.3 us, and not the 1.6 of the forecast.

*The rivals.* The port's wait did come, 2.56 us beside a fd of 2.61, and 0.16 where rsc ran ahead of fd; the rule of the Trainium skill (SBUF — State Buffer, section SBUF: two separate sides), by which the loser blocks for the other's whole instruction, agrees. But I priced it at the full 3.0 us at the end, and e3 and e5, which take it away, gain 0.2% and 0.4%, neither told from nothing. POOL as the bound didn't come about where I looked for it: of each 10 us from 60 to 90 it is busy for

```profile
60.00:70.00 10.00, 10.00 (x128) 6.88 (x127) 9.77 (x18) 9.82 (x22) 9.51 (x11) 1.00 1.02 201
70.00:80.00 10.00, 9.36 (x108) 6.18 (x106) 9.43 (x22) 8.87 (x21) 8.28 (x10) 1.00 0.99 198
80.00:90.00 10.00, 10.00 (x113) 6.29 (x111) 9.96 (x16) 9.60 (x20) 8.72 (x10) 1.00 0.92 199
```

9.51, 8.28 and 8.72 us. It is full earlier, from 30 to 40 us, in after and in e4 alike (10.00 us each); whether its longer list makes the 1.2 us above was not tried. The loss that came, a load's price and with it the late filter, was a term of my sum and no rival.
